# A head's key copies in causal attention: high and low part in two planes of one tile

## The chip, the cores and the metric

One Trainium2 chip, of which the program uses one core. The metric is the device time of one execution in microseconds; a kernel's time is the median of its runs.

## The reference, cut to what matters

Three stages run one after the other on inputs of batch 4 and sequence 768: a linear attention with a decaying state (8 heads of 48), an MLP with a convolution and a gate (384 to 1024 and back), and a mixture of four attention experts with head size 64, of which each token takes the best two. The change lies in the third stage, for each expert `e` (called a head below):

```python
for e in range(E):
    q = x @ wq[e]
    k = x @ wk[e]
    v = x @ wv[e]
    scores = scale * (q @ k.transpose(0, 2, 1))
    scores = np.where(causal, -1000000000.0, scores)
    scores = scores - scores.max(-1, keepdims=True)
    a = np.exp(scores)
    a /= a.sum(-1, keepdims=True) + 1e-09
    ye = a @ v @ wo[e]
    ...
```

## The kernel before, in words

The first two stages (`phase1`) run from the start to about 388 us, with an order of instructions written out by hand; the class `Attention` is the third and runs from about 344 us to the end. Within `Attention` the order on each engine is not written out: a scheduler of the framework lays it down when the program is built, from the order of the source and an estimate of the times. Each engine then works in that order, and SyncE's queue SP, which issues all DMAs, does so too.

`Attention.run` goes over eight projections `i` (four batches, two pairs of heads each) and sixteen units `j` (a projection and one half of its query rows). `proj(i)` makes queries and keys of a pair of heads, and for the first pair of a batch also loads `x` (`xload`, line 805: three loads of 384 KB through two buffers, each split by ScalarE and GpSimd into two parts `xs`) and makes the values. `softs(j)` makes scores and exponentials (`soft`, line 890), `tail(j - 1)` transposes them, multiplies by the values and projects the output, which line 970 stores.

TensorE multiplies in fp32r. For precision each operand is split into a high part, which the format holds, and a low part, the rest. `qk_group` (line 815) computes one half of the sequence for two heads at once: head `j` lies in partitions 64 j to 64 j + 63. ScalarE writes the high part `hi` (line 829: `qh` or `kh`), VectorE the low part `lo` (line 830: `ql` or `kl`). After the second half the parts are copied from SBUF to SBUF by DMA, so that each head has tiles of 128 partitions:

- queries `sq`: the high part in one half of the partitions, the low part in the other (lines 837 and 838)
- keys `sk`: the high part in both halves (lines 837 and 838, four transfers for the two heads)
- keys `sl`: the low part in both halves (lines 846 and 847, four transfers), from a pool `lp` of its own

One matmul of `sq` with `sk` then gives (high + low of q) times the high part of k, and one with `sl` adds (high + low of q) times the low part. `soft` issues these two in turn into one accumulator `st` (lines 898 to 901), and VectorE reads `st` at line 913 when both are done. Each key transfer moves 64 partitions of 3072 bytes, which are 192 KB. On SP the loads of `x` and the stores of `ot` stand in the same queue as the copies.

Of the kernel before, what the change touches and what calls it, by code (L numbers as in the profile page):

```python
# [11 lines left out]
F32R = mybir.dt.float32r  # L12
# [8 lines left out]
B, H, S, D = 4, 8, 768, 48  # L21
# [27 lines left out]
def _f(ap):  # L49
    return ap.bitcast(F32)  # L50
# [712 lines left out]
class Attention:  # L763
# [31 lines left out]
    def open_right(self):  # L795
        tc = self.tc
        R = lambda n, b, **k: self.right.enter_context(tc.tile_pool(name=n, bufs=b, side="right", **k))
        self.ap = R("ap", 2)
        self.sp = R("sp", 3)
        self.lp = R("lp", 2)  # L800
        self.ps_s = R("ps2_s", 2, space=PSUM)

    P3 = ((0, 0), (0, 1), (1, 0))
# [11 lines left out]
    def qk_group(self, xs, hl, n, p, h):  # L815
        nc = self.nc
        w, sc = (self.wq, -0.125) if n == "q" else (self.wk, 1.0)
        if h == 0:
            hl[n] = [self.qp.tile([128, S], F32R, name=n + z, bufs=1) for z in "hl"]
        hi, lo = hl[n]  # L820
        s = slice(h * HT, (h + 1) * HT)
        pt = self.ps_m.tile([128, 512], F32, name="m")
        m = 0
        for i in range(3):
            for wi, xi in self.P3:
                nc.tensor.matmul(pt[:, 0:HT], w[wi][:, i, p * 128:(p + 1) * 128], xs[xi][:, i, s],  # L826
                                 start=(m == 0), stop=(m == 8))
                m += 1
        nc.scalar.activation(hi[:, s], pt[:, 0:HT], AF.Copy, scale=sc)
        nc.vector.scalar_tensor_tensor(lo[:, s], pt[:, 0:HT], sc, _f(hi[:, s]), op0=OP.mult, op1=OP.subtract)  # L830
        if h == 0:
            return
        ts = []
        for j in range(2):
            o, z = slice(64 * j, 64 * j + 64), slice(64 - 64 * j, 128 - 64 * j)
            t = self.qp.tile([128, S], F32R, name=f"s{n}{j}")
            nc.sync.dma_start(_f(t[o]), _f(hi[o]))
            nc.sync.dma_start(_f(t[z]), _f((lo if n == "q" else hi)[o]))
            ts.append(t)
        hl["s" + n] = ts  # L840
        if n == "k":
            hl["sl"] = []
            for j in range(2):
                o, z = slice(64 * j, 64 * j + 64), slice(64 - 64 * j, 128 - 64 * j)
                t = self.lp.tile([128, S], F32R, name=f"sl{j}")
                nc.sync.dma_start(_f(t[o]), _f(lo[o]))
                nc.sync.dma_start(_f(t[z]), _f(lo[o]))
                hl["sl"].append(t)

    def v_group(self, xs, V, t):  # L850
        nc = self.nc
# [38 lines left out]
    def soft(self, hl, j, qi, A, rs):  # L890

        nc, sp = self.nc, self.sp
        W = (qi + 1) * C
        nb = 1 if W <= 512 else 2
        n = max(W, 256) // nb
        q = hl["sq"][j]
        st = self.ps_s.tile([128, 2, 512], F32, name="st")
        for z in range(nb):
            for i, k in enumerate((hl["sk"][j], hl["sl"][j])):
                nc.tensor.matmul(st[:, z, 0:n], q[:, qi * C:(qi + 1) * C], k[:, z * n:(z + 1) * n], start=(i == 0),  # L900
                                 stop=(i == 1))
        w = W // nb
        mn = sp.tile([128, 1], F32, name="mn")
        at = A[:, self.OFF[qi]:self.OFF[qi] + W]
        if nb == 2:
            sm = sp.tile([128, 2, HT], F32, name="sm")
            o3, i3 = sm[:, :, 0:w], st[:, :, 0:w]
            m3 = self.mask[:, S - W:].rearrange("p (z w) -> p z w", z=2)
            at = at.rearrange("p (z w) -> p z w", z=2)
        else:  # L910
            sm = sp.tile([128, 2 * HT], F32, name="sm")
            o3, i3, m3 = sm[:, 0:W], st[:, 0, 0:W], self.mask[:, S - W:]
        nc.vector.tensor_tensor_reduce(o3, i3, m3, 1.0, 3e38, op0=OP.add, op1=OP.min, accum_out=mn)  # L913
        nc.scalar.activation(at, o3, AF.Exp, bias=mn, scale=-1.0, accum_out=rs[:, qi % 3:qi % 3 + 1])  # L914
# [263 lines left out]
```

## Time and profile before

| What | us |
| --- | --- |
| median of 3 runs | 637.61 |
| lowest and highest run | 636.97 and 640.27 |
| the profiled execution | 635.43 |
| its span in the profile | 633.7 |

The profile is of one execution, whose time stands beside its span: some 1.7 us lie around the span. The execution is faster than the median of the runs. PE is TensorE's matmuls, PEld its weight loads, DVE VectorE, ACT ScalarE, POOL GpSimd, SP SyncE; SPq is its queue of DMA issues. `st<-sl,sq` is an operation that writes the tile `st` and reads `sl` and `sq`. Times in the views count from the start of the span.

### The profile page before, as it was taken

What the parts mean: (1) busy time and instruction counts of PE and PEld (TensorE: products, weight loads), DVE (VectorE), ACT (ScalarE), POOL (GpSimd) and SP (SyncE); (2) the same over time, 40 slices, a digit from 0 to 9 for tenths busy, and PEclk for the clock granted to TensorE, in tenths of its full rate; (3) what the DMA queues carried; (4) which work ended last, traced back from release to release, by engine and by line L of the source; (5) the groups of instructions that cost most, each with busy time, mean ns of one, the idle gap of its engine ahead of it and who ended that gap; (6) DMA issues with size and microseconds to landing.
All of it is one profiled execution on the core that took longest, in us unless ns stands there. A gap on an engine that the chain in (4) does not pass through costs nothing.

```text
span 633.7 us, 11479 instructions
## 1 busy us (share of the span) xinstructions
PE 589.2 (93%) x4038; PEld 469.0 (74%) x4038; DVE 494.6 (78%) x1123; ACT 374.8 (59%) x945; POOL 146.5 (23%) x210
## 2 busy tenths in 40 slices
PE   5778899999999999999999999899998998999896
PEld 4657677777777777777777777687988887978654
DVE  6999999999999898999955642978749773865471
ACT  4875555656656777676555634575657555655452
POOL 2222332342323232323206400210021002004060
PEclk9778999999999999999999999999999999899899
DMA  8666454554554767645125541742365226422502
GB/s 284 214 213 223 153 185 157 157 160 151 152 155 145 213 204 242 205 142 159 52 76 155 170 105 38 199 125 53 88 177 135 75 64 162 117 56 66 138 2 80
DMA packets 34963, 89.47 MB, mean 141 GB/s; under 512 B 5456, under 2 KB 16208, under 8 KB 34896
## 3 DMA queue, kind: packets, MB, share of 16 engines
q1 hardware_dynamic: 34896, 88.64, 47.0%
q8 instruction: 34, 0.56, 0.4%
q14 instruction: 33, 0.27, 0.1%
HBM read 50.82 MB, written 9.44 MB: 95 GB/s over the span
## 4 chain that ended last, share of the span: by engine, by line
PE 56%; DVE 18%; DMA 9%; ACT 7%; issue 4%; POOL 3%; SPq 2%; DVEq 0%; ACTq 0%; POOLq 0%
PE x L444 11%; PE hs L394 9%; PE m L826 6%; PE st L900 6%; PE m L950 5%; PE t L934 4%; PE m L962 4%; PE m L856 3%; DMA x<-x 3%; DMA rkv<-in_rkv 3%; PE sc L289 2%; DVE Ss L336 2%; DVE Dp L232 2%; PE m L350 2%; DVE Fp L239 2%
## 5 line engine op out<-in xcount | busy, mean ns | idle before, releaser
L444 PE MATMUL x<-gt,wout 128*128 128x386 f32 (+1 forms) x384 | 133.5, 485 | 0.0
L394 PE MATMUL hs<-X,win 128*128 128x384 f32 (+1 forms) x576 | 118.5, 350 | 3.8 <-ACT ht L398 3.2
L394 PEld LDWEIGHTS hs<-X,win 128*128 128x128 f32 x576 | 98.3, 188 | 12.5 <-ACT ht L398 5.9
L444 PEld LDWEIGHTS x<-gt,wout 128*128 128x128 f32 x384 | 71.9, 189 | 35.1
L421 ACT ACTIVATE st<-ct 128x382 f32<-128x382 f32 (+1 forms) x64 | 33.5, 524 | 82.8 <-DVE ct L415 45.2
L914 ACT ACTIVATE A<-sm,mn 128x128 f32<-128x128 f32 (+5 forms) x96 | 63.8, 665 | 26.9 <-DVE mn L913 26.2
L913 DVE CUSTOM_DVE_ANT_0 sm<-st,mask 128x128 f32<-128x128 f32 (+5 forms) x96 | 58.1, 618 | 18.8 <-PE st L900 16.2
L934 PE MATMUL t<-ident,A 128*128 128x128 f32 x336 | 54.0, 277 | 1.7 <-ACT T L938 0.8
L271 POOL TENSOR_SCALAR_AFFINE_SELECT AT<-e 128x384 f32<-128x384 f32 x52 | 25.9, 522 | 118.1 <-DVE e L261 112.3
L431 DVE SCALAR_TENSOR_TENSOR gt<-st,ht 128x382 f32<-128x382 f32 (+1 forms) x64 | 41.1, 643 | 11.7 <-ACT st L421 8.5
L900 PE MATMUL st<-sk,sq 128*128 128x384 f32 (+3 forms) x128 | 44.7, 360 | 3.6 <-DVE mn L913 2.8
L940 DVE COPY T<-t 128x128 f32<-128x128 f32 (+3 forms) x64 | 32.3, 504 | 20.0 <-PE t L934 19.5
L934 PEld LDWEIGHTS t<-ident,A 128*128 128x128 f32 x336 | 40.8, 141 | 7.9 <-issue 2.2
L900 PE MATMUL st<-sl,sq 128*128 128x384 f32 (+3 forms) x128 | 41.6, 338 | 5.0 <-DMA sl<-kl 4.9
L289 PEld LDWEIGHTS sc<-Q,K 64*128 64x128 f32 x384 | 28.7, 207 | 22.4 <-DVE AT L295 9.0
L938 ACT ACTIVATE T<-t 128x512 f32<-128x512 f32 (+3 forms) x64 | 28.6, 446 | 27.0 <-PE t L934 22.3
L950 PE MATMUL m<-T,V 128*64 128x384 f32 (+2 forms) x288 | 43.8, 423 | 0.0
L289 PE MATMUL sc<-Q,K 64*128 64x128 f32 x384 | 35.9, 313 | 7.8 <-DVE AT L295 7.7
L812 POOL TENSOR_TENSOR xs<-x,xs 128x768 fp32r<-128x768 f32 x12 | 22.5, 1891 | 86.7 <-ACT xs L811 86.7
L398 ACT ACTIVATE ht<-hs 128x384 f32<-128x384 f32 (+1 forms) x64 | 31.2, 487 | 18.9 <-PE hs L394 18.8
L402 ACT ACTIVATE ct<-ht,cwk 128x382 f32<-128x382 f32 (+1 forms) x64 | 39.5, 616 | 2.0
L232 DVE TENSOR_TENSOR_SCAN Dp<-wkr,cD 128x387 f32<-128x387 f32 x32 | 36.9, 1153 | 4.0 <-POOL cD L151 4.0
(132 smaller groups left out, 1169.6 us busy)
## 6 DMA issues: line engine op xcount, KB each, us to landing
wkr<-in_wkr SPq DMA_DIRECT2D x31, 578.0 KB, 3.9
rkv<-in_rkv SPq DMA_DIRECT2D x22, 480.0 KB, 4.6
rawt<-in_win SPq DMA_DIRECT2D x8, 768.0 KB, 7.0
rawt<-in_wout SPq DMA_DIRECT2D x8, 768.0 KB, 4.3
sk<-kh SPq DMA_DIRECT2D x32, 192.0 KB, 3.3
sl<-kl SPq DMA_DIRECT2D x32, 192.0 KB, 4.0
x<-x SPq DMA_DIRECT2D x12, 384.0 KB, 4.3
out_dram<-ot SPq DMA_DIRECT2D x24, 192.0 KB, 1.9
```

Of the source, the lines that this page charges most:

```text
L232: nc.vector.tensor_tensor_scan(fl(t["Dp"]), t["w"][:, 0:NW], fl(cD), 0.0, op0=OP.mult, op1=OP.add)
L289: nc.tensor.matmul(sc[j][:, c], t["K"][p, c], t["Q"][p, c], start=True, stop=True)
L394: nc.tensor.matmul(hs[:, 0:N], win[wi][:, f // 2, i, (f % 2) * 128:(f % 2 + 1) * 128], x[:, i, xi], start=(n == 0), stop=(n == 8))
L402: nc.scalar.activation(ct, ht[:, o:o + N], AF.Copy, scale=w[:, 1, f:f + 1])
L431: nc.vector.scalar_tensor_tensor(gt, st, 1.0, ht[:, o:o + N], op0=OP.add, op1=OP.mult)
L444: nc.tensor.matmul(acc[0][i][:, 0:N], wout[:, f, i * 128:(i + 1) * 128], gt, start=(f == 0), stop=(f == NF - 1))
L826: nc.tensor.matmul(pt[:, 0:HT], w[wi][:, i, p * 128:(p + 1) * 128], xs[xi][:, i, s], start=(m == 0), stop=(m == 8))
L900: nc.tensor.matmul(st[:, z, 0:n], q[:, qi * C:(qi + 1) * C], k[:, z * n:(z + 1) * n], start=(i == 0), stop=(i == 1))
L913: nc.vector.tensor_tensor_reduce(o3, i3, m3, 1.0, 3e38, op0=OP.add, op1=OP.min, accum_out=mn)
L914: nc.scalar.activation(at, o3, AF.Exp, bias=mn, scale=-1.0, accum_out=rs[:, qi % 3:qi % 3 + 1])
L934: nc.tensor.transpose(pt[:, ki - k0], at[:, ki * C:(ki + 1) * C], self.ident)
L950: nc.tensor.matmul(po[o, lo:HT], V[:, ki, (2 * p + j) * 64:(2 * p + j + 1) * 64], Ts[j][:, ki, lo:], start=(ki == 0), stop=(ki == n - 1))
```

## The change

`hl["q"]` and `hl["k"]` become one tile each of two planes (plane 0 is the high part, plane 1 the low part), so that both parts of one partition lie one behind the other, 6144 bytes. The key tile `sk` of a head gets the two planes as well, and takes in what `sl` held. A head's keys are then copied by two transfers (one for each half of the partitions) of 64 partitions and both planes, 384 KB each, where there were four of 192 KB. The transfers of a projection come in the order: head 0, both halves; head 1, both halves. The pool `lp` goes. The four transfers of the queries keep their contents. `soft` reads the planes of `sk` where it read `sk` and `sl`.

```diff
--- before.py
+++ after.py
@@ -797,7 +797,6 @@
         R = lambda n, b, **k: self.right.enter_context(tc.tile_pool(name=n, bufs=b, side="right", **k))
         self.ap = R("ap", 2)
         self.sp = R("sp", 3)
-        self.lp = R("lp", 2)
         self.ps_s = R("ps2_s", 2, space=PSUM)
 
     P3 = ((0, 0), (0, 1), (1, 0))
@@ -816,8 +815,8 @@
         nc = self.nc
         w, sc = (self.wq, -0.125) if n == "q" else (self.wk, 1.0)
         if h == 0:
-            hl[n] = [self.qp.tile([128, S], F32R, name=n + z, bufs=1) for z in "hl"]
-        hi, lo = hl[n]
+            hl[n] = self.qp.tile([128, 2, S], F32R, name=n + "hl", bufs=1)
+        hi, lo = hl[n][:, 0], hl[n][:, 1]
         s = slice(h * HT, (h + 1) * HT)
         pt = self.ps_m.tile([128, 512], F32, name="m")
         m = 0
@@ -830,22 +829,14 @@
         nc.vector.scalar_tensor_tensor(lo[:, s], pt[:, 0:HT], sc, _f(hi[:, s]), op0=OP.mult, op1=OP.subtract)
         if h == 0:
             return
-        ts = []
+
+        hl["s" + n] = []
         for j in range(2):
             o, z = slice(64 * j, 64 * j + 64), slice(64 - 64 * j, 128 - 64 * j)
-            t = self.qp.tile([128, S], F32R, name=f"s{n}{j}")
-            nc.sync.dma_start(_f(t[o]), _f(hi[o]))
-            nc.sync.dma_start(_f(t[z]), _f((lo if n == "q" else hi)[o]))
-            ts.append(t)
-        hl["s" + n] = ts
-        if n == "k":
-            hl["sl"] = []
-            for j in range(2):
-                o, z = slice(64 * j, 64 * j + 64), slice(64 - 64 * j, 128 - 64 * j)
-                t = self.lp.tile([128, S], F32R, name=f"sl{j}")
-                nc.sync.dma_start(_f(t[o]), _f(lo[o]))
-                nc.sync.dma_start(_f(t[z]), _f(lo[o]))
-                hl["sl"].append(t)
+            t = self.qp.tile([128, S] if n == "q" else [128, 2, S], F32R, name=f"s{n}{j}")
+            nc.sync.dma_start(_f(t[o]), _f(hi[o] if n == "q" else hl[n][o]))
+            nc.sync.dma_start(_f(t[z]), _f(lo[o] if n == "q" else hl[n][o]))
+            hl["s" + n].append(t)
 
     def v_group(self, xs, V, t):
         nc = self.nc
@@ -896,7 +887,7 @@
         q = hl["sq"][j]
         st = self.ps_s.tile([128, 2, 512], F32, name="st")
         for z in range(nb):
-            for i, k in enumerate((hl["sk"][j], hl["sl"][j])):
+            for i, k in enumerate((hl["sk"][j][:, 0], hl["sk"][j][:, 1])):
                 nc.tensor.matmul(st[:, z, 0:n], q[:, qi * C:(qi + 1) * C], k[:, z * n:(z + 1) * n], start=(i == 0),
                                  stop=(i == 1))
         w = W // nb
```

## Rows read from the trace of the kernel before

**Rows 1.** The page, parts 1 (busy time) and 4 (chain that ended last).

```profile
PE 589.2 (93%) x4038; PEld 469.0 (74%) x4038; DVE 494.6 (78%) x1123; ACT 374.8 (59%) x945; POOL 146.5 (23%) x210
...
PE 56%; DVE 18%; DMA 9%; ACT 7%; issue 4%; POOL 3%; SPq 2%; DVEq 0%; ACTq 0%; POOLq 0%
```

**Rows 2.** Waits: who waited for whom: us in total, times, longest us.

```profile
PE st L900 <- DMA sl<-kl: 4.9, 4, 2.4
...
PE m L826 <- ACT xs L811: 3.8, 3, 2.6
```

**Rows 3.** The chain in order of time: start us, us, what.

```profile
407.35 4.57 DMA x<-x
...
532.19 4.49 DMA x<-x
...
552.32 5.16 DMA sl<-kl
...
590.23 4.65 DMA sl<-kl
```

**Rows 4.** The page, part 6, DMA issues: KB each, us to landing.

```profile
sl<-kl SPq DMA_DIRECT2D x32, 192.0 KB, 4.0
```

**Rows 5.** Timeline at 587: start us, us, engine, line, operation [idle <- releaser].

```profile
586.44 0.49 ACT L829 ACTIVATE kh<-m 128x384 fp32r<-128x384 f32 x1 [1.02 <-PE m L826]
...
586.96 0.46 SPq L837 DMA_DIRECT2D sk<-kh  x1
...
587.00 0.55 DVE L830 SCALAR_TENSOR_TENSOR kl<-m,kh 128x384 fp32r<-128x384 f32 x1
...
591.38 0.62 PE L900 MATMUL st<-sk,sq 128*128 128x512 f32 x2
...
595.01 1.03 PE L900 MATMUL st<-sl,sq 128*128 128x512 f32 x2 [2.36 <-DMA sl<-kl]
```

**Rows 6.** Stretches: busy time of each engine, then PEclk, DMA share, GB/s.

```profile
588.00:595.00 7.00, 4.66 (x35) 3.46 (x34) 2.50 (x5) 2.18 (x4) 0.00 (x0) 1.00 0.98 229
595.00:598.25 3.25, 3.23 (x10) 2.18 (x10) 1.53 (x4) 0.78 (x2) 0.00 (x0) 0.50 0.34 115
598.50:600.00 1.50, 1.50 (x11) 1.31 (x11) 0.65 (x1) 1.07 (x4) 0.00 (x0) 1.00 0.00 0
```

**Rows 7.** Stretch 410 to 412, mostly a load of x.

```profile
410.00:412.00 2.00, 2.00 (x16) 1.35 (x15) 1.99 (x7) 0.05 (x1) 0.00 (x0) 1.00 0.87 326
```

**Rows 8.** DMA issue of the key copy at 588.76.

```profile
sk<-kh SPq DMA_DIRECT2D x1, 192.0 KB, 4.3
```

**Rows 9.** Timeline at 549 to 558, and the stretch behind it.

```profile
549.79 0.55 DVE L830 SCALAR_TENSOR_TENSOR kl<-m,kh 128x384 fp32r<-128x384 f32 x1
...
553.34 0.48 PE L900 MATMUL st<-sk,sq 128*128 128x256 f32 x2
...
557.61 0.36 PE L900 MATMUL st<-sl,sq 128*128 128x256 f32 x1 [0.87 <-DMA sl<-kl]
...
557.60:562.00 4.40, 4.39 (x30) 2.82 (x32) 2.60 (x18) 1.58 (x6) 0.00 (x0) 1.00 0.01 2
```

**Rows 10.** Timeline at 401 and at 525: kh, kl, and PE's wait for xs.

```profile
401.13 0.49 ACT L829 ACTIVATE kh<-m 128x384 fp32r<-128x384 f32 x1 [0.96 <-PE m L826]
...
403.08 0.55 DVE L830 SCALAR_TENSOR_TENSOR kl<-m,kh 128x384 fp32r<-128x384 f32 x1
...
524.25 0.49 ACT L829 ACTIVATE kh<-m 128x384 fp32r<-128x384 f32 x1 [1.01 <-PE m L826]
...
525.29 0.55 DVE L830 SCALAR_TENSOR_TENSOR kl<-m,kh 128x384 fp32r<-128x384 f32 x1
...
537.61 0.61 PE L826 MATMUL m<-xs,wq 128*128 128x384 f32 x2 [2.59 <-ACT xs L811]
```

**Rows 11.** Timeline at 487 to 491: kl, and the first score products.

```profile
487.39 0.55 DVE L830 SCALAR_TENSOR_TENSOR kl<-m,kh 128x384 fp32r<-128x384 f32 x1
...
490.94 0.48 PE L900 MATMUL st<-sk,sq 128*128 128x256 f32 x2
```

## The prediction, made before the changed kernel was run

> **What bounds the kernel now.** I read the page first. TensorE is busy for 93% of the span, and the chain that ended last runs over PE for 56% and over DMA for 9% [rows 1]. So a transfer matters only where the chain passes through it. The waits show which transfers do: PE waited 4.9 us in 4 waits for the low part `sl`, and 3.8 us in 3 waits for `xs`, which is made from the loads of `x` [rows 2]. The pieces of the chain give the places: two pieces are copies of `sl` (5.16 us at 552 and 4.65 us at 590) and three are loads of `x`, of which the first and the last are shown [rows 3]. SyncE issues the loads of `x` behind the copies of the keys, so both ends of this change meet in one queue.
>
> I name the eight projections by the time at which their key copies start. Today a projection issues eight transfers of 192 KB for the keys: four of the high part, then four of the low part [rows 4]. At 587 the high part is written from 586.44 to 586.93, the first copy is issued at 586.96, the low part is ready at 587.55, and PE takes up the low product at 595.01 after 2.36 us without work [rows 5]. Only the first head's pair is needed there, yet its low copies are the fifth and sixth of the eight. During this stretch the DMA engines are 98% busy at 229 GB/s [rows 6]: the transfers are not waiting to be issued, they wait for each other's bytes. After the stall PE runs for 3.25 us at a granted clock of 0.50 (1.2 GHz), then at 1.00 (2.4 GHz) again [rows 6].
>
> **The change, part by part.** *Removed:* four key transfers per projection, 32 in all, and the pool `lp`. *Added:* nothing on an engine; the remaining four carry 384 KB each. *Moved:* the first head's low part comes from places five and six to the first pair, and the first transfer now waits for VectorE's `kl` as well as for ScalarE's `kh`.
>
> The bytes are the same, so I take the drain as the same. The nearest row with another rate is a 128-partition load of `x`: 326 GB/s at 87% busy [rows 7]. It could say that 384 KB transfers drain faster, but that row also differs in that all 128 partitions take part, while a key copy reads 64 and writes 64. Bounds for a 192 KB unit are 0.86 us (229 GB/s) and 0.60 us (326 GB/s); I take 0.86, since its row is the same kind of copy, and keep the other as a rival. The Trainium skill, SBUF — State Buffer, section "Door 1: The DMA port swizzle", says that partitions of one 64-half reach 8 of 16 ports, with an asymptote of about 218 GB/s; this speaks against any gain from larger transfers. By it a unit would be 0.90 us (an estimate from that page), and the trace's 229 GB/s lies close.
>
> *The first pair.* In the new order two transfers hold four units. Today's fourth unit was issued at 588.76 and landed 4.3 us later [rows 8], at 593.06, which is 6.1 us after the first issue. I use 6.1 for the new pair, counted from the end of `kl`.
> - At 587: 587.6 + 6.1 = 593.7, against 590.23 + 4.65 = 594.88 today [rows 3, 5]. That is 1.2 us earlier and leaves some 1.2 us of the 2.36 us stall. The slow stretch did 3.25 us of work at half clock, so 1.6 us go if PE stays at full clock. It did after the shorter stall of 0.87 us at 557 (granted clock 1.00 behind it) [rows 9], so I count it. Sum 2.8; bounds 1.2 (the clock falls all the same) and 4.0 (no stall left).
> - At 549: `kl` ends at 550.34 [rows 9], so the pair lands at 556.5 against 557.48 today. The whole 0.87 us of PE's wait goes; bounds 0 and 0.9. There is no load of `x` between this place and the end, so both gains reach the end.
>
> *What is queued behind.* SP waits longer before the first key copy, and the loads of `x` (with the stores of `ot`) stand behind it. With the drain unchanged the whole stream moves by the time between `kh` and `kl`:
> - At 401: `kh` ends at 401.62, `kl` at 403.63, since VectorE had other work [rows 10]. The load of `x` issued at 407.35 would land up to 2.0 us later. Bounds 0 (VectorE's order comes out with `kl` earlier, or SP, free after four issues, sends `x` sooner) and 2.0; I take 1.0, the middle, as no row decides.
> - At 525: 524.74 against 525.84 [rows 10]. PE already waits 2.59 us there for `xs` [rows 10], so 1.1 us is added. Bounds 0 and 1.1.
> - At 464: `kl` follows at once, as at 587, so 0.6 us, the 0.61 of [rows 5]. Bounds 0 and 0.6.
>
> The `sl` waits that vanish at 464 and 525 bring nothing, because the load of `x` ends later than they do. The other three projections have their softmax well behind the copies, and cost nothing; if that cover were gone, each would show up to the 2 us of the first pair. Fewer issues on SyncE are worth nothing by themselves: the DMA engines stay busy through them [rows 6]. The matmuls read the same rows in the same count. The larger tile takes space that the finished first phase gave up.
>
> *Sum:* 0.9 + 2.8 gained, 1.0 + 1.1 + 0.6 lost: 1.0 us faster. The profiled execution took 635.43 us (span 633.7 and 1.7 around it), 2.2 below the median of 637.61, so 634.4 of its kind and **636.6 us** for the median. With the bounds, this case reaches from 632.7 (4.9 gained, nothing lost) to 640.1 (1.2 gained, 3.7 lost). A measurement of this kernel tells about 0.5% (3.2 us) from no change.
>
> **The rivals.**
> *The loads of `x` keep their time.* The instruction order on each engine is made anew when the program is built, and SP issues half as many key copies; `x` could slip in front of them. Then only the gains stay: 3.7 us, 633.9. For it: SP sat behind these copies until 407.35 [rows 3]. Against it: the stream is bound by bytes [rows 6].
> *Larger transfers drain faster.* At 0.60 us a unit the pair lands 1.0 us earlier and the stream ends 8 x 0.26 = 2.1 us earlier, more than the delays of 0.6 to 2.0. Then the stall at 587 goes (4.0), the one at 549 too (0.9), and the loads of `x` land 0.1, 1.0 and 1.5 us earlier (2.1 less the delays); 7.5 in all, 630.1. Against it: the half-partition copies [rows 6, 7]. The Trainium skill, DMA: Bandwidth & Descriptors, section "Rules for kernel authors", would have it so: for the highest bandwidth it asks to coalesce small transfers into large ones, of 128 partitions and 1 MiB or more. No run here shows yet a 64-partition copy of 384 KB.
> *Slower: the first product waits for both planes.* Today PE runs the high product while the low copies are still under way: at 553.34 and 557.61 [rows 9], and at 490.94 with `kl` ready only at 487.94 [rows 11]. If the first product keeps its place on PE, which works in order, it blocks what stands behind it until the pair lands: at 487.9 + 6.1 = 494.0 instead of 490.94, 3.1 us; at 556.5 instead of 553.34, 3.2 less the 0.87 saved, 2.3 us. With the three delays of `x` at full price (3.7) that is 9.1 us, 646.7. It decides from the point where more than a third of this is not covered (3.2 us). Against it: the order is made anew with the later copy in view, and would put other work first.
> *The change does not do what it says:* if the two planes are cut into the same 3 KB rows and finish together, nothing moves: 637.6.
>
> **How the numbers follow.** Forecast 0.42, `x` keeps its time 0.17, faster drain 0.17, first product blocked 0.19, no effect 0.05. Faster by over 0.5% (below 634.4): 0.17 of the drain, 0.13 of the second case, 0.03 of the forecast's edge: 0.33. Slower by over 0.5% (above 640.8): 0.19, the blocked product. The rest is 0.48. The range goes from the drain case, 630.1, to 641.5, which leaves out most of the slower case and a little below. The likeliest case's own range is 632.7 to 640.1.
>
> **What would show it.** Right: key transfers x32 at 384 KB; the stall before the first score products at the last projection near 1 us or none, with no stretch at 0.50 behind it; the wait at 549 gone; waits for `xs` as long as before or longer; 220 to 240 GB/s while keys are copied. Wrong: a rate near 300 GB/s there; PE waits of 2 us and more for the merged `sk` in front of other work; waits for `xs` that shrink; or a chain that no longer passes through these places, because the engines' orders came out otherwise.

## The result, and the profile after

The changed kernel takes 642.26 us (16 runs, 638.98 to 643.88) against 637.12 us for the one before (16 runs): a ratio of 1.0088, with an interval of 1.0068 to 1.0108. It is **slower by 0.9%**, some 5.1 us. The two profiled executions show the same: 641.17 us (span 639.2) against 635.43 us (span 633.7).

The page of the kernel after, parts 1, 4 and 6 (for [rows 1, 4]):

```profile
PE 594.3 (93%) x4038; PEld 473.6 (74%) x4038; DVE 493.3 (77%) x1123; ACT 374.8 (59%) x945; POOL 146.5 (23%) x210
...
PE 59%; DVE 18%; DMA 8%; ACT 8%; issue 3%; POOL 2%; SPq 1%; POOLq 0%; ACTq 0%; DVEq 0%
...
sk<-khl SPq DMA_DIRECT2D x32, 384.0 KB, 6.3
```

The change did what it says: 32 transfers of 384 KB, and as many instructions on every engine as before. PE is busy 5.1 us longer for the same 4038 matmuls, which points to the clock, but only in part to the change: 2.7 of the 5.1 us lie before 340 us, in the stages that the change doesn't touch (PE is busy there for 320.38 us against 317.64). The waits (for [rows 2]) and the chain (for [rows 3]; start us, us, what):

```profile
ACT xs L810 <- DMA x<-x: 19.0, 5, 6.4
PE m L825 <- ACT xs L810: 6.2, 3, 3.0
PE st L891 <- issue: 2.8, 3, 2.3
PE st L891 <- DMA sk<-khl: 0.8, 2, 0.4
```

```profile
541.40 0.48 PE L891 MATMUL st<-sk,sq 128*128 128x256 f32 x2 [1.43 <-DMA out_dram<-ot]
```

```profile
403.93 1.47 SPq L837
405.44 1.96 SPq L838
407.86 5.41 DMA x<-x
...
473.34 1.41 SPq L961
474.84 4.72 DMA x<-x
...
538.51 1.33 SPq L961
539.93 4.33 DMA x<-x
```

PE's waits for keys look as if they were gone (4.9 us for the low part before, 0.8 us for the merged `sk`), but two more stand under other names. The 2.3 us under "issue" end at 599.34, when the pair copied at 592.58 and 593.09 has landed. The 1.43 us at 541.40 end just after the last key copy, issued at 533.97, has landed (7.2 us later, at 541.2). The waits for `xs` grew from 3.8 to 6.2 us. Every DMA piece of the attention stage that the chain shows is now a load of `x`, and in front of each stands SP's own queue, busy with issuing key copies (L837, L838) or stores of `ot` (L961). The timeline of SP at the projection of 464 (for the same stretch of before, the second fence) shows why:

```profile
466.31 0.46 SPq L837 DMA_DIRECT2D sk<-khl  x1
466.83 0.59 SPq L838 DMA_DIRECT2D sk<-khl  x1
467.47 1.34 SPq L837 DMA_DIRECT2D sk<-khl  x1
468.85 1.91 SPq L838 DMA_DIRECT2D sk<-khl  x1
470.86 3.88 SPq L961 DMA_DIRECT2D out_dram<-ot  x2
474.84 0.90 SPq L809 DMA_DIRECT2D x<-x  x2
```

```profile
464.28 0.46 SPq L837 DMA_DIRECT2D sk<-kh  x1
...
469.13 0.70 SPq L847 DMA_DIRECT2D sl<-kl  x1
469.94 1.51 SPq L970 DMA_DIRECT2D out_dram<-ot  x2
471.54 1.03 SPq L810 DMA_DIRECT2D x<-x  x2
```

The four key copies hold SP for 4.55 us together, less than the 5.66 us of the eight before, though the third and fourth take 1.34 and 1.91 us. The two stores behind them take 3.88 us in place of 1.51. The load of `x` goes out 8.53 us after the first key copy in place of 7.26. What that costs stands in the stretches (columns as in [rows 6]; the third is of before) and in PE's timeline:

```profile
478.00:480.00 2.00, 0.00 (x0) 0.00 (x0) 0.20 (x1) 0.41 (x1) 0.00 (x0) 0.94 0.52 196
...
479.80:486.60 6.80, 6.12 (x20) 5.39 (x21) 4.54 (x15) 5.15 (x15) 1.82 (x1) 0.50 0.22 63
...
473.00:486.00 13.00, 11.33 (x71) 10.26 (x70) 10.76 (x35) 9.28 (x26) 1.83 (x1) 1.00 0.56 166
```

```profile
480.48 1.01 PE L825 MATMUL m<-xs,wq 128*128 128x384 f32 x2 [3.02 <-ACT xs L810]
```

PE stands still for 3.02 us, and after that works for 6.8 us at a granted clock of 0.50 (1.2 GHz). Before, the stretch of 473 to 486 us, with the same loads and waits of 0.72 and 0.86 us, ran at 1.00 (2.4 GHz).

Read by stages, from the end of one projection's high part (`kh`, line 829 before, 828 after) to the next, the kernel after loses 2.1 us between the projections of 401 and 423, 4.1 us between those of 464 and 487, and 1.0 us between those of 525 and 549. These are the three stretches that begin with a load of `x` on the chain. It gains 1.6 us between 549 and 587, and loses 0.5 us after that. Up to 401 it is 0.8 us ahead. With 0.1 us in the other stretches that makes the 5.5 us between the two spans.

### The profile page after: what moved, and what is told of

Same layout as the page of the kernel before. It is cut to its first block, busy times and chain, and to the rows that moved or that the text cites. A ratio compares the mean times of both kernels' runs of the same rounds, so it can differ in the third digit from the quotient of the medians.

```text
span 639.2 us, 11439 instructions
## 1 busy us (share of the span) xinstructions
PE 594.3 (93%) x4038; PEld 473.6 (74%) x4038; DVE 493.3 (77%) x1123; ACT 374.8 (59%) x945; POOL 146.5 (23%) x210
## 4 chain that ended last, share of the span: by engine, by line
PE 59%; DVE 18%; DMA 8%; ACT 8%; issue 3%; POOL 2%; SPq 1%; POOLq 0%; ACTq 0%; DVEq 0%
PE x L444 11%; PE hs L394 9%; PE m L825 7%; PE m L941 6%; PE st L891 6%; PE t L925 5%; PE m L847 4%; PE m L953 4%; DMA wkr<-in_wkr 3%; PE sc L289 3%; DMA x<-x 2%; PE m L350 2%; PE m L356 2%; DVE Ss L336 2%; DMA rkv<-in_rkv 2%
## 5 line engine op out<-in xcount | busy, mean ns | idle before, releaser
L394 PE MATMUL hs<-X,win 128*128 128x384 f32 (+1 forms) x576 | 120.2, 353 | 2.8 <-ACT ht L398 2.2
L394 PEld LDWEIGHTS hs<-X,win 128*128 128x128 f32 x576 | 100.0, 191 | 11.1 <-ACT ht L398 4.2
L891 PE MATMUL st<-sk,sq 128*128 128x384 f32 (+3 forms) x256 | 59.9, 356 | 6.8 <-issue 2.8
L891 PEld LDWEIGHTS st<-sk,sq 128*128 128x128 f32 x256 | 43.1, 201 | 13.1 <-issue 6.0
```

Of the source, the lines that this page charges most:

```text
L394: nc.tensor.matmul(hs[:, 0:N], win[wi][:, f // 2, i, (f % 2) * 128:(f % 2 + 1) * 128], x[:, i, xi], start=(n == 0), stop=(n == 8))
```

## The experiments

In each kernel the scheduler lays down the order of the engines anew. To change one thing at a time, most kernels here are **held to an order**: PE, VectorE, ScalarE and GpSimd keep the order of the kernel before, or that of the kernel after, through dependences that add no wait between instructions of one engine. All ratios are to the kernel before, measured beside them.

### The planes and the order, apart

Nothing in the source of these two changes but the order: the kernel after in before's order, and the kernel before in after's order.

> The changed kernel, with VectorE, ScalarE, GpSimd and TensorE held to the order of instructions of the kernel before (SyncE's queue has that order already). Stream theory (the key copies start later, because they wait for the low part, and 384 KB transfers drain slower, 195 against 215 GB/s, so that the loads of x behind them come later): it stays slow, 641 to 645 us, with the loads of x landing 2 to 4 us later than in the kernel before. Order theory (the loss lies in the order of instructions that was made anew): it comes back to 635 to 638 us.

> The kernel before, with the same four engines held to the order of the changed kernel. Stream theory: its transfers are the old ones, so 635 to 638 us. Order theory: 641 to 644 us.

The kernel after in before's order took 653.62 us (1.026, interval 1.0221 to 1.0299), more than either of my theories gave; the kernel before in after's order 635.67 us (0.9993, 0.9965 to 1.002). So the new order costs nothing by itself. It even shields the change: without it the planes would cost 16.5 us and not 5. PE's timeline of the first kernel at 404:

```profile
404.10 0.55 PE L925 MATMUL t<-ident,A 128*128 128x128 f32 x3 [0.19 <-ACT T L929]
409.41 0.55 PE L891 MATMUL st<-sk,sq 128*128 128x256 f32 x1 [4.76 <-DMA sk<-khl]
```

In the fixed order the first score product blocks PE for 4.76 us, until both planes are there. Before, it waited 0.63 us at this place, for the high part alone.

### Late start, and size of the transfers

The first kernel is the one before, in its own order, with one wait added: the copies of the high part are held until the low part is written. The second is the kernel after in before's order, with each 384 KB transfer cut into its two planes and each piece held until the low part is written. In the code `...` stands for lines left out.

```diff
-            nc.sync.dma_start(_f(t[o]), _f(hi[o]))
+            d = nc.sync.dma_start(_f(t[o]), _f(hi[o]))
+            if n == "k":
+                self.tc.add_manual_dep(d.ins, low.ins.name, late, reason="late")
...
```

```diff
-            nc.sync.dma_start(_f(t[o]), _f(hl[n][o]))
-            nc.sync.dma_start(_f(t[z]), _f(hl[n][o]))
+            for to in (o, z):
+                for y in range(2):
+                    d = nc.sync.dma_start(_f(t[to, y]), _f(hl[n][o, y]))
...
```

> The kernel before, in its own order on all engines, with eight transfers of 192 KB as ever, but the high copies also wait for the low part. If the late start alone makes the loss: 640 to 642 us. If it is the slower drain or the order: 637 to 639 us; the predicted delays of 0.6 to 2.0 us at the three loads of x would make 3.7 us at most.

> The changed kernel in the order of the kernel before, each 384 KB transfer cut into two of 192 KB (one for each plane) in the same sequence, all of them behind the low part. If size makes the drain slower: the last copy lands 8.8 to 9.1 us after the first issue instead of 9.4 to 9.8, and the time is 1 to 2 us below that of the same order with four transfers. If the sequence (both transfers of a head read the same half of the partitions) does it: 9.4 to 9.8 us as with four, and the same time.

The late start took 642.58 us (1.0099, 1.0059 to 1.0139): by itself, with nothing else changed, it costs as much as the whole change. That the two sums are equal doesn't make it the same loss: the late start stands here in before's order, and there PE waits 2.65 us at 407.54 for the high part, a wait that the kernel after does not have. The cut transfers took 642.84 us (1.0088, 1.0055 to 1.0121), 10.8 us less than the same order with whole ones (653.62), where I had expected 1 to 2. They start as late, and SP comes to `x` as late at 464 (8.47 us after the first copy, 8.46 with whole ones). So the 16.5 us in a fixed order are some 5.5 for the late start and some 11 for whole transfers. PE's waits at the score products, 17.0 us with whole transfers and 9.5 us with cut ones, fit a product that can't begin before both planes have landed.

### Does the sequence slow the stream?

At the projection of 423, where nothing stands behind, before's last key copy is issued at 428.17 and lands 4.0 us later, which is 8.8 us after the issue of the first; after's is issued at 427.81 and lands 6.9 us later, 9.5 us after the first. The sequence has changed too: 768 KB in a row are now read from the same 64 partitions (head by head), where before it was 384 KB, and then the other half's turn (in alternation). This kernel, in after's order, brings the alternation back with whole transfers:

```diff
...
+        for m in range(4):
+            j, y = (m // 2, m % 2) if n == "q" else (m % 2, m // 2)
+            o, to = H[j][0], H[j][y]
+            nc.sync.dma_start(_f(hl["s" + n][j][to]), _f((hi, lo)[y][o] if n == "q" else hl[n][o]))
```

> After's kernel, its four compute engines held to after's order, with the four 384 KB key transfers in another sequence: the two that read different halves of the partitions follow each other (head 0's own half, head 1's own half, then the swapped ones). If the slower drain comes from two transfers in a row that read the same 64 partitions: the last lands 8.8 to 9.1 us after the first issue in place of 9.4 to 9.8, as before's eight do. If it comes from the size of the transfers: 9.4 to 9.8 as in after. In both cases head 0 is complete with the third landing, at 7.3 to 7.6 in place of 5.75 us, so the first product waits some 1.7 us longer at each of the seven projections, of which what the engine does meanwhile hides a part: 642 to 650 us against after's 642.3.

646.8 us (1.0164, 1.0128 to 1.02), and the last copy lands 9.3 us after the first where nothing stands behind: alternating the halves speeds up the stream a little at most, and a head that is complete later costs 4.5 us. The cut transfers above end at 9.2 us. Together the four kernels cross the two suspects. Six us from the middle of this stream, in the order before (192 KB, halves in alternation), cut transfers (192 KB, head by head), this kernel (384 KB, in alternation), after (384 KB, head by head):

```profile
425.00:431.00 6.00, 6.00 (x48) 5.83 (x47) 5.80 (x15) 3.30 (x8) 0.00 (x0) 1.00 0.98 231
...
430.00:436.00 6.00, 6.00 (x50) 5.96 (x50) 5.08 (x15) 4.44 (x11) 0.00 (x0) 1.00 0.98 217
...
427.40:433.40 6.00, 4.93 (x40) 4.72 (x38) 4.32 (x13) 3.71 (x13) 0.00 (x0) 1.00 0.98 220
...
427.00:433.00 6.00, 6.00 (x50) 5.96 (x49) 4.68 (x15) 3.69 (x12) 0.00 (x0) 1.00 0.98 213
```

Both carry a part: head by head costs 14 GB/s at 192 KB and 7 at 384 KB, the larger size 11 and 4. (Three other kernels with before's transfers move 230 to 233 GB/s here, two others with after's 211 and 213.) The time until SP comes to the load of `x` at 464 goes with the sequence: 7.26 us in before, 7.71 with the late start and 7.66 here, all in alternation; 8.53 in after, 8.46 in before's order and 8.47 with the cut transfers, all head by head. Four transfers or eight make no such difference. (One value stands against it: 8.24 us in before with the buffer of the next section.)

### The loads of x out of the way

A batch has three loads of `x` and two buffers for them. In both kernels the first two go out long before, and the third waits until ScalarE and GpSimd have split the first. That one stands behind the key copies on SP, and it is the one on the chain. With a third buffer it goes out with the others, one batch earlier:

```diff
+    def xget(self, b):
+        self.X = [self.xp.tile([128, S], F32, name="x", bufs=3) for i in range(3)]
+        for i in range(3):
+            self.nc.sync.dma_start(self.X[i], self.x2[:, b, i])
...
+            if p == 1 and b + 1 < B:
+                self.xget(b + 1)
```

> After's kernel, its four compute engines held to after's order; only the loads of the next x are issued earlier (from a third buffer, ahead of the copies of the projection before), so that they no longer stand on SP behind the key transfers. If the loss of 5 us sits in the loads of x behind a stalled SP (between the projections with loads behind them after lost 2.15, 4.1 and 1.0 us on before): 634 to 638, the waits of the projection's matmuls for xs (6.2 us in after) fall below 2 us. If the later first product is what counts, wherever x is: 640 to 643, and the wait moves to the score tiles.

> Before's kernel in before's order with the loads of x issued early in the same way. Measures what the loads of x behind the copies cost before the change (PE's waits for xs 3.8 us there): 632 to 635 if that wait is on the path, 636 to 638 if what is gained is waited out at the score tiles of the same projection.

The kernel after, held to its own order, fell to **630.21 us** (0.9901, 0.9865 to 0.9936), the kernel before, held to its own, to **629.37 us** (0.9877, 0.9844 to 0.9909). Both gained more than expected, and what had been 0.88% between them is 0.24%, inside the width of either interval. So the loss of the change, in its own order, sat in these three loads. Stretches of the kernel after with the buffer, then its waits:

```profile
470.00:486.00 16.00, 14.59 (x96) 13.44 (x95) 12.37 (x45) 11.09 (x30) 1.82 (x1) 1.00 0.73 199
533.00:549.00 16.00, 14.40 (x95) 13.34 (x95) 14.35 (x51) 11.03 (x31) 1.82 (x1) 1.00 0.42 105
```

```profile
PE st L896 <- DMA out_dram<-ot: 2.0, 2, 1.2
ACT xs L815 <- DMA x<-x: 2.0, 1, 2.0
...
PE st L896 <- DMA sk<-khl: 1.5, 3, 0.6
```

There is no wait of PE for `xs` any more, and both stretches keep the full clock. The key copies themselves are as in the kernel after (32 of 384 KB, 6.2 us to landing).

### What the buffer doesn't hide

The same buffer in two of the kernels above, in before's order: the planes, and the late start.

> After's planes with its four compute engines held to before's order, as in the run that took 653.6 us, and with the third buffer for x, so that a batch's third load no longer waits for the cast of its first and stands ahead of the key transfers. If nothing but that load carries the cost of the planes: 630 to 633, as after's order gives with the buffer (630.2). If the first product, which has to wait for both planes, costs by itself where the order keeps no other work for the gap: 640 to 645, with 6 us or more of PE's idle time at score tiles that wait for sk, in pieces at every projection.

> Before's kernel in before's order, the copies of the high part held until the low part is written (642.6 us by itself, against 637.1), and with the third buffer for x. If the late start costs only because it pushes back the load of x on SP: 629 to 631, no more than before's kernel with the buffer (629.4). If the score tiles wait for the keys themselves: 633 to 636, with the difference in idle time at score tiles.

The planes took 647.44 us (1.0172, 1.0131 to 1.0213), more than I expected even of the second theory. The late start took 638.22 us (1.0038, 1.0008 to 1.0068), also more than its second theory: 1.6% above the kernel before with the buffer. So in before's order the late start costs by itself, some 9 us even with `x` out of the way; the theory that it costs through `x` alone is wrong for that order. PE's waits in the late start (first two lines) and in the planes:

```profile
PE st L910 <- DMA sl<-kl: 8.9, 5, 3.1
PE st L910 <- DMA sk<-kh: 3.4, 3, 2.6
```

```profile
PE st L896 <- DMA sk<-khl: 12.7, 4, 4.9
PE st L896 <- issue: 4.6, 2, 2.7
```

The two lines of the planes make 17.3 us. In after's order with the buffer the waits of the score products are 1.5 us for `sk`, 2.6 under "issue" and 2.0 under the stores, 6.1 us at most. The new order puts other work before the first product and is worth 647.4 - 630.2 = 17 us here, waits and clock together; it didn't do the same for `x`, on which the next projection hangs.

### Less to copy, and the head-first sequence with the buffer

The first two kernels keep the planes, but ScalarE and VectorE write each head's own half of the keys straight into its head tile, so that only the swapped half is copied: two transfers of 384 KB in place of four, the second kernel with the third buffer as well. Both have an order of their own.

```diff
+            for (o, z), t in zip(H, hl["sk"]):
+                nc.scalar.activation(t[o, 0, s], pt[o, 0:HT], AF.Copy)
+            for (o, z), t in zip(H, hl["sk"]):
+                nc.vector.tensor_tensor(t[o, 1, s], pt[o, 0:HT], _f(t[o, 0, s]), op=OP.subtract)
...
+                nc.sync.dma_start(_f(t[z]), _f(t[o]))
```

> After's two planes, but ACT and DVE write each head's own half of the keys straight into its head tile (two instructions of 64 partitions each in place of one of 128), so that two transfers of 384 KB remain in place of four, and the tile between is gone; orders remade by the scheduler. Priced from after: the first pair is complete when the first transfer lands, 3.65 us after its issue in place of 5.75, the last at 5.8 in place of 9.4 to 9.8, SP is free for the loads of x some 3.5 us earlier; the extra instructions are 4 on ACT and 4 on DVE for each of 8 projections, some 0.3 us each at the end of a projection's path. If the key transfers are what after lost: 630 to 636. If the longer path through ACT and DVE eats it: 638 to 643.

> The direct write of the keys into the head tiles (two transfers of 384 KB; 628.8 us by itself) together with the third buffer for x. What is left there of waits of the projections for xs is 1.0 us at one and 0.5 at another, with part of a half-clock stretch behind them: 624 to 628 if they go and nothing takes their place; 628 to 631 if the order that the scheduler makes costs what the buffer brings.

628.84 us (0.9883, 0.985 to 0.9917), and 630.61 us with the buffer (0.9916, 0.9891 to 0.994). The instructions added are 16 on each of the two engines, not the number that I gave. With half the bytes PE's waits for `xs` are down to 1.6 us; part of that can be the order, in which the load of `x` at 401 now goes out ahead of the key copies. The buffer takes these waits too, but the time is no lower, and the two intervals overlap.

The last kernel is the one before, in its order, with the buffer and its eight transfers of 192 KB in another sequence: per head the high part twice, then the low part twice. Nothing waits for the low part at the start.

> Before's four tiles and eight 192 KB transfers, in before's order of the compute engines, with the third buffer for x (629.4), and the transfers issued head by head (head 0's two of the high part, its two of the low part, then head 1's) with no wait for the low part at the start: what the change was for, without its large transfers and without the late start. Head 0 is then complete with the fourth landing, 5.5 us after the first issue in place of 7.2 for its sixth, head 1's high part comes at 7.2 in place of 5.5. If the waits of the scores for the low part (1.6, 1.6, 0.8 and 2.3 us of PE's idle time there) are on the path: 624 to 628. If they are waited out elsewhere or head 1 takes their place: 629 to 632.

**623.38 us** (0.9808, 0.977 to 0.9846): below the expected 624 to 628, and 4 to 6 us below the same kernel without the new sequence (4.4 by the ratios, 6.0 by the medians). It beats both kernels. Its SP timeline and PE's at the last projection:

```profile
578.31 0.46 SPq L842 DMA_DIRECT2D sk<-kh  x1
578.82 0.59 SPq L843 DMA_DIRECT2D sk<-kh  x1
579.50 0.55 SPq L847 DMA_DIRECT2D sl<-kl  x1
580.10 0.59 SPq L848 DMA_DIRECT2D sl<-kl  x1
580.74 0.89 SPq L842 DMA_DIRECT2D sk<-kh  x1
```

```profile
584.84 0.65 PE L901 MATMUL st<-sl,sq 128*128 128x512 f32 x2 [0.82 <-DMA sl<-kl]
585.33 0.31 PE L901 MATMUL st<-sk,sq 128*128 128x320 f32 x1
```

The stall there is 0.82 us, against 2.36 before [rows 5] and 2.32 with the buffer alone, and the clock doesn't fall, as the stretch behind it shows:

```profile
585.00:589.00 4.00, 4.00 (x24) 3.02 (x25) 2.80 (x6) 2.39 (x6) 0.00 (x0) 1.00 0.74 187
```

The scheduler gave SP this sequence at five of the eight projections; at the one of 401 the order stayed as it was, and at two the first head's low part came fourth and fifth. So what the change was after, an early low part, is worth having, and was there to be had without larger transfers. The sequence was run only together with the buffer; what it brings without it is not shown.

## Why the prediction was wrong

I forecast 636.6 us, with 641.5 as the upper end; it came out at 642.26. Two steps failed. The larger is **"What is queued behind"**, and in it the sentence "With the drain unchanged the whole stream moves by the time between `kh` and `kl`", with the three terms 1.0, 1.1 and 0.6 (2.7 in all). The smaller is the 2.8 us gained at 587, in **"The first pair"**. Counted from the end of `kh` to the landing of `x` on the chain:

| projection | before | after | later by | priced at |
| --- | --- | --- | --- | --- |
| 401 | 407.35 + 4.57 - 401.62 = 10.3 | 407.86 + 5.41 - 400.80 = 12.5 | 2.2 | 1.0 |
| 464 | 471.54 + 4.32 - 464.25 = 11.6 | 474.84 + 4.72 - 465.67 = 13.9 | 2.3 | 0.6 |
| 525 | 532.19 + 4.49 - 524.74 = 11.9 | 539.93 + 4.33 - 530.28 = 14.0 | 2.0 | 1.1 |

That is 6.5 us in place of 2.7. The mechanism was the right one and the size was off, for three reasons. At 401 I took the middle between 0 and 2.0; the copies started the whole 2.0 later, and what `x` gained by going out 0.6 us sooner behind them it lost by taking 5.41 us in place of 4.57. At 464 and 525 SP came to `x` 1.3 and 1.1 us later by its own work, since the stores behind the copies took it longer to issue. I had written that "Fewer issues on SyncE are worth nothing by themselves"; that sentence held, but I didn't ask whether the new sequence could hold SP up, and by the runs above it is the sequence, not the size, that goes with the delay. And the stream isn't unchanged. Over the key copies at 464 and at 587, with the stores between them and part of the loads, it moved 215 and 211 GB/s before and 195 and 193 after, as these stretches show, before first:

```profile
464.30:473.30 9.00, 7.73 (x54) 6.50 (x54) 3.73 (x11) 4.23 (x9) 3.62 (x2) 1.00 0.87 215
586.90:596.00 9.10, 6.74 (x45) 5.43 (x44) 3.33 (x8) 2.70 (x6) 0.00 (x0) 0.94 0.86 211
```

```profile
466.30:476.00 9.70, 8.81 (x62) 7.30 (x60) 4.03 (x11) 4.87 (x12) 3.61 (x2) 1.00 0.86 195
592.60:602.00 9.40, 7.13 (x43) 5.72 (x42) 3.14 (x7) 2.87 (x6) 0.00 (x0) 0.85 0.87 193
```

The second thing missing from the loss was the clock. I counted it as a gain at 587, and not as a loss behind a longer wait for `xs`. At 480 PE was busy for 6.12 us at 1.2 GHz, by my estimate 3.1 us more than the same work takes at 2.4 GHz. That is one execution; how often the clock falls there in the others is not shown. At 525 the clock makes no difference: in both kernels some 3.4 us at 1.2 GHz follow the wait for `xs` (540.4 to 543.8 before, 544.6 to 548.0 after).

Over the two spans the forecast was 1.0 us gained and the result 5.5 lost. Of these 6.5 us, 4.5 lie in the three stretches with a load of `x` (7.2 lost in place of 2.7) and 3.3 at 587 (0.5 lost in place of 2.8 gained). Against that stand 0.7 us more than counted at 549 and the 0.8 us by which after is ahead at 401.

The other steps:

- *The first pair at 549:* right. The pair lands 5.8 us after its first issue (6.1 taken), and PE's wait of 0.87 us there is gone.
- *The first pair at 587:* mostly wrong. 2.8 us were counted. There the second transfer of the pair is issued at 593.09 and takes 6.2 us, 6.7 after the first issue. PE's wait is 2.27 us in place of 2.36, and the clock falls behind it as before:

```profile
599.34 1.99 PE L891 MATMUL st<-sk,sq 128*128 128x512 f32 x5 [2.27 <-issue]
...
599.20:602.60 3.40, 3.26 (x12) 2.93 (x12) 1.66 (x5) 0.82 (x2) 0.00 (x0) 0.50 0.89 227
```

  I let the high products run ahead of the pair, as they do today, though the rival three paragraphs on says that they can't.
- *Rival "the loads of x keep their time":* wrong, as the table shows. *Rival "larger transfers drain faster":* wrong; with the new sequence they drained 8 to 9% slower, and at the same sequence 2 to 5%. By the Trainium skill, DMA: Bandwidth & Descriptors, section "Rules for kernel authors", coalescing pays because transfers under 64 KB are mostly overhead; both sizes here, 192 and 384 KB, lie above that, and the runs show no gain. By the Trainium skill, SBUF — State Buffer, section "Door 1: The DMA port swizzle", 64 partitions reach about 218 GB/s. The trace agrees where the copies go head by head (217 and 213 GB/s in mid-stream); in alternation the stream of 192 KB copies went above it, at 231 GB/s, and there the measurement decides.
- *Rival "the first product waits for both planes":* its mechanism is real. In before's order it stood in the trace at 4.76 us, and with the late start it cost 16.5 us, more than the 9.1 that I priced. The reason that I gave against it held too: in its own order the kernel is 11 us faster. It named the right side, by another way.

## What to carry to other kernels

When a change moves or merges transfers, list what stands behind them in the same queue, and price that with the queue's own issue time, not with the bytes alone. A load that waits for a buffer, and so stands behind other transfers, is worth a buffer early: here it gave 8 us before the change and 12 after it, though nothing where half the key bytes were gone already. The Trainium skill, DMA: Bandwidth & Descriptors, section "Rules for kernel authors", asks to issue a transfer early and to wait late; these runs agree. And before two parts are merged into one transfer, ask whether the reader can start on the first part alone: 192 KB pieces in the right sequence, with the buffer, did what the 384 KB transfers were meant to do.

## What the runs showed of the hardware

- The time SP takes to issue a transfer depends on what is under way. A 384 KB copy took 0.46 and 0.59 us as first and second, 1.34 and 1.91 us as third and fourth, and a 192 KB store behind them some 1.9 us, against 0.34 us with the queue empty. Before, no key copy of 192 KB took more than 0.95 us. Until SP was through copies and stores at 464, the sequence counted more than the size: 7.26 to 7.71 us in alternation and 8.46 to 8.53 head by head, with 192 as with 384 KB (and 8.24 once in alternation, with the buffer).
- 64-partition copies inside SBUF moved 231 GB/s in mid-stream as 192 KB in alternation, 220 as 384 KB in alternation, 217 as 192 KB head by head and 213 as 384 KB head by head. One profiled execution of each stands behind this; why the sequence counts stayed open.
- In before and after, a wait of PE of 3.02 us was followed by 6.8 us at 1.2 GHz, and waits of 2.36 and 2.27 us by some 3.4 us; in the last kernel one of 0.82 us by none. The length of the wait alone doesn't decide: in the kernel before in after's order PE waited 2.72 us and stayed at 2.4 GHz, as it did behind 2.40 and 2.99 us in the late start, where 1.74 us at 480.05 were followed by 3.4 us at 1.2 GHz. The first of these:

```profile
593.65 0.47 PE L900 MATMUL st<-sl,sq 128*128 128x512 f32 x1 [2.72 <-DMA sl<-kl]
...
593.60:597.00 3.40, 3.35 (x18) 2.56 (x19) 1.78 (x5) 2.11 (x5) 0.00 (x0) 1.00 0.36 117
```
